# Attention with pooled keys, then an MLP: the first batch loaded and turned one head pair at a time

## The chip, the cores and the metric

The kernel runs on one core of a Trainium2 chip. The metric is device microseconds of one execution, taken as the median of several. Before the change it is 308.15 us (4 runs, 307.08 to 308.27). The engines are TensorE (PE; PEld is its weight load), VectorE (DVE), ScalarE (ACT), GpSimd (POOL) and SyncE (SP), which only issues DMAs here. Each engine runs its own instructions in order, and waits on semaphores for the others. ACT and POOL issue DMAs too, each on a queue of its own; all queues are served by the same 16 DMA engines. A load that POOL issues may convert float32 to bfloat16 on the way.

## The reference

Eight batches of 8 heads, 576 positions, head dimension 64. Keys and values are averaged over groups of 8 positions, so that each head has 72 of them; softmax attention follows, and its output (4608 tokens of 512 features) goes through an MLP with hidden size 2048 and the activation h - tanh(h).

```python
k_p = k.reshape(B, H, Sp, pool, D).mean(axis=3)      # 576 -> 72 rows
v_p = v.reshape(B, H, Sp, pool, D).mean(axis=3)
scores = scale * np.matmul(q, k_p.transpose(0, 1, 3, 2))
attn = softmax(scores)
x = np.matmul(attn, v_p)                             # then heads side by side
h = x @ w_in                                         # (4608, 512) @ (512, 2048)
out = (h - np.tanh(h)) @ w_out                       # (4608, 2048) @ (2048, 512)
```

## The kernel before

**Layout of k and v.** Two heads make a pair; a pair has 2 x 72 = 144 pooled rows (`PR`). The pair t, of four (`NM`), puts its first 128 rows in `k_raw[:, t, :]`, one row per partition, eight positions of 64 numbers each. The 16 rows left over (`LO`) of all four pairs share a fifth slice, `k_raw[:, NM, :]`: pair t has partitions 32t to 32t+15, the others hold zero. `v_raw` has the same layout. `load_main` (L101) loads the main rows, `load_left` (L105) the leftover rows, with one DMA per pair.

**Pooling.** `pool_k` (L186 to L194) adds the eight positions in three steps and writes the sum twice, side by side, into `kd`. TensorE turns `kd` by a matmul with the identity (`turn_tile`, L243), and `kb_main` and `kb_left` copy the result out of PSUM into `KB` so that two heads share a 128-column block with zeros where they must not meet. `VB` is built from pooled v: each pair's rows are written twice, multiplied by a mask that keeps the one or the other head (`v_spread`, L216 and L224); its last column holds the pool size, so that the attention matmul gives the softmax denominator too.

**Attention of a batch.** `score_mms` (L282) multiplies a block of `KB` with the turned q of that pair; the leftover rows of all pairs make a fifth tile, each pair in its 32 partitions. The exponential goes into `E` (L312). `av_half` (L330) gives 128 tokens of four heads: two matmuls for the two pairs, a third for their leftover rows. A reciprocal and a product on VectorE make `x_sb` (L343, L344). `x_pe_transpose` (L374) turns it into `xT` (copy on ScalarE, L381), the MLP's input.

**The MLP.** Tokens go in 9 groups of 512. `mlp_h_mms` (L412) accumulates one of 16 hidden blocks over four feature blocks, so heads 0-3 give the first two of them and heads 4-7 the last two; `mlp_h_act` takes tanh on ScalarE (L423) and the difference on VectorE (L425). `mlp_o` (L440) is the second layer. While TensorE works on group g, GpSimd pools k and v of a later batch and casts q.

**What sets the order.** The order of each engine's instructions is that of the program text, written out by hand (`manual_schedule`). Waits are placed by the framework, from the tiles that an instruction reads and writes. Two more kinds of waits matter here. DMAs take their completion semaphores in turn from a small set of lanes (eight for SP and ACT together, eight for POOL), so a DMA waits for the one that used its lane before. And `after` adds waits by hand: batch 1's k loads wait for the second of four chunks of `w1`.

**The start.** Batch 0 has nothing to hide behind. SP loads k pairs 0 and 1, the four leftover pieces, then pairs 2 and 3; ACT loads q in two halves; POOL loads v as bfloat16 straight into `v_bf` (a view of `v_raw[0]`), then `w1` in four chunks and the first of `w2`. VectorE pools k, TensorE turns k and q, pools v by eight matmuls with the identity as weights (L596), and multiplies zeros in between (`warm_pe`, L511), results of which nobody reads. The MLP's first matmuls on batch 0 are those of the first two feature blocks of hidden blocks 0 to 4. Then come group 0's remaining hidden blocks; group 0's second layer (16 steps u) is interleaved with the attention of batch 1: its k is turned after u=0 (`k_transpose`), its q from u=3, and `av` starts at u=9.

Of the kernel before, what the change touches and what calls it, by code (L numbers as in the profile page):

```python
# [8 lines left out]
FP32 = mybir.dt.float32  # L9
BF16 = mybir.dt.bfloat16  # L10
# [27 lines left out]
def kernel(  # L38
# [34 lines left out]
    xT = const.tile([128, NFB, T], BF16, name="xT")  # L73
    ident = const.tile([128, 128], BF16, name="ident")
    mask = const.tile([128, 3 * NM, 1], FP32, name="mask")
    k_raw = [const.tile([128, NT, POOL * D], FP32, name=f"k_raw{i}") for i in range(2)]
# [26 lines left out]
    def load_left(src, dst, b):  # L103
# [3 lines left out]
        ]  # L107

    def load_k(b):
        return [load_main(k_pairs, k_raw[b % 2], b, 0, NM)] + load_left(  # L110
            k_pairs, k_raw[b % 2], b
        )

# [88 lines left out]
    def pool_v(b, eng):  # L202
        r = v_raw[b % 2].rearrange("p t (j d) -> p t j d", d=D)
        eng.tensor_tensor(  # L204
            out=r[:, :, 0:4, :], in0=r[:, :, 0:4, :], in1=r[:, :, 4:8, :], op=ALU.add
        )
        eng.tensor_tensor(  # L207
            out=r[:, :, 0:2, :], in0=r[:, :, 0:2, :], in1=r[:, :, 2:4, :], op=ALU.add
        )
        eng.tensor_tensor(  # L210
            out=r[:, :, 0, :], in0=r[:, :, 0, :], in1=r[:, :, 1, :], op=ALU.add
        )
        v_spread(VB[b % 2], r[:, :, 0:1, :], eng)

    def v_spread(vb, vs, eng):
        eng.tensor_tensor(  # L216
            out=vb[:, 0 : 2 * NM, 0:D].rearrange("p (t s) d -> p t s d", s=2),
            in0=vs[:, 0:NM, :, :].to_broadcast([128, NM, 2, D]),
            in1=mask[:, 0 : 2 * NM, :]
            .rearrange("p (t s) o -> p t s o", s=2)  # L220
            .to_broadcast([128, NM, 2, D]),
            op=ALU.mult,
        )
        eng.tensor_tensor(  # L224
            out=vb[:, 2 * NM :, 0:D],
            in0=vs[:, NM, :, :].to_broadcast([128, NM, D]),
            in1=mask[:, 2 * NM :, :].to_broadcast([128, NM, D]),
            op=ALU.mult,
        )
# [6 lines left out]
    def kb_left(kb, ps, eng):  # L236
        eng(
            out=kb[D:128, :].rearrange("p (t x) -> p t x", x=KP)[:, :, 128 : 128 + LO],
            in_=ps[D:128, :].rearrange("p (t x) -> p t x", x=32)[:, :, 0:LO],
        )  # L240
# [35 lines left out]

    def score_mms(b, t, dst, c0, c1):
        for m in range(NM) if t == NM else (t,):
            o = m * KP + (128 if t == NM else 0)
# [25 lines left out]
    def scores_wide(b, ts):  # L305
# [3 lines left out]
        for t in ts:  # L309
            ps = ps_any([128, QA], FP32, "s_ps")  # L310
            score_mms(b, t, ps[:, :], 0, QA)
            nc.scalar.activation(out=E[:, t, 0:QA], in_=ps[:, :], func=ACT.Exp, scale=SCALE)  # L312

    def scores_tail(b):
        ps = ps_any([128, NT, QT], FP32, "s_ps")
        for t in range(NT):
            score_mms(b, t, ps[:, t, :], QA, S)
        nc.scalar.activation(
            out=E_tiles[b][:, :, QA:S], in_=ps[:, :, :], func=ACT.Exp, scale=SCALE
        )  # L320

    def av_half(b, blk, half, x_sb, alloc):
        E = E_tiles[b]
# [3 lines left out]
        for n in range(3):  # L327
            t = 2 * half + n if n < 2 else NM
            s0 = 2 * t if n < 2 else 2 * NM + 2 * half
            nc.tensor.matmul(  # L330
                ps[:, 2 * n : 2 * n + 2, :].rearrange("p h d -> p (h d)")
                if n < 2
                else ps.rearrange("p (a s) d -> p a s d", s=2)[:, :, 1, :],
                lhsT=E[:, t, c0 : c0 + 128],
                rhs=vb[:, s0 : s0 + 2, :].rearrange("p h d -> p (h d)")
                if n < 2
                else vb[:, s0 : s0 + 2, :],
                start=(n == 0),
# [185 lines left out]
    nc.vector.memset(k_raw[0][:, NM, :], 0.0)  # L524
    load_main(k_pairs, k_raw[0], 0, 0, 2)
    load_q0(0, 4)
    load_left(k_pairs, k_raw[0], 0)
    load_main(k_pairs, k_raw[0], 0, 2, 4)
    load_q0(4, 8)
    nc.scalar.dma_start(out=t0[:QT, :, R, :], in_=q[0, :, QA:S, :].rearrange("h p d -> p h d"))  # L530

    warm_pe(13)
    nc.vector.memset(warm[:, :], 0.0)
# [3 lines left out]
    make_identity(nc, ident)  # L537
    nc.gpsimd.memset(v_bf[:, NM, :], 0.0)
    nc.gpsimd.memset(q_bf[64:128, R, :, :], 0.0)
# [18 lines left out]
    nc.gpsimd.dma_start(out=v_bf[:, 0:NM, :], in_=v_pairs[0, 0:128, :, :])  # L558
    for t in range(NM):
        nc.gpsimd.dma_start(  # L560
            out=v_bf[32 * t : 32 * t + LO, NM, :], in_=v_pairs[0, 128:PR, t, :]
        )
    for c in range(4):
        load_w1(c)
    load_w2(0)
    nc.gpsimd.memset(k_raw[1][:, NM, :], 0.0)
    nc.gpsimd.memset(v_raw[1][:, NM, :], 0.0)
    nc.gpsimd.memset(v_raw[0][:, NM, :], 0.0)
# [16 lines left out]

    pool_k(0, nc.vector, 0, 2)
    def q_turn(eng, h0, h1):
# [5 lines left out]
    def v_pe_pool():  # L593
        ps = ps_any([128, NT, 1, D], FP32, "v_ps")
        for j in range(POOL):
            nc.tensor.matmul(  # L596
                ps[:, :, 0, :],
                lhsT=ident[:, :],
                rhs=v_bf[:, :, j * D : (j + 1) * D],
                start=(j == 0),  # L600
                stop=(j == POOL - 1),
            )
        v_spread(VB[0], ps, nc.vector)

# [3 lines left out]
    ps_all = ps_any  # L608
    q_turn(nc.vector.tensor_copy, 0, 4)
    k_turn(0, 2)  # L610
    warm_pe(1)
    q_pe_transpose(0, (0, 1), "act")
    pool_k(0, nc.vector, 4, 5)
    pool_k(0, nc.vector, 2, 4)
    warm_pe(3)
    scores_wide(0, (0, 1))
    q_turn(nc.scalar.copy, 4, 8)
    warm_pe(5)
    k_turn_left()
    k_turn(2, 4)  # L620
    q_pe_transpose(0, (2, 3), "act")
    v_pe_pool()
    scores_wide(0, (2, 3, 4))
    xs = [new_x() for _ in range(4)]
    gts = []
    warm_pe(2)
    av_half(0, 0, 0, xs[0], ps_all)
    av_half(0, 1, 0, xs[1], ps_all)
    warm_pe(1)
    x_pe_transpose(0, 0, xs[0], (0, 2))  # L630
    av_half(0, 2, 0, xs[2], ps_all)
    warm_pe(1)
    x_pe_transpose(0, 1, xs[1], (0, 2))
    av_half(0, 3, 0, xs[3], ps_all)
    warm_pe(1)
    x_pe_transpose(0, 2, xs[2], (0, 2))
    ps_any = ps_b1
    av_half(0, 0, 1, xs[0], ps_any)
    warm_pe(1)
    x_pe_transpose(0, 3, xs[3], (0, 2))  # L640
    av_half(0, 1, 1, xs[1], ps_any)
    av_half(0, 2, 1, xs[2], lambda sh, dt, name: ps_h.tile(sh, dt, name=name, tag="hT_ps"))
    mlp_h_mms(0, 0, 0, 2)
    x_pe_transpose(0, 0, xs[0], (2, 4))
    av_half(0, 3, 1, xs[3], ps_any)
    mlp_h_mms(0, 1, 0, 2)
    x_pe_transpose(0, 1, xs[1], (2, 4))
    mlp_h_mms(0, 2, 0, 2, (ps_o, "o_ps"))
    x_pe_transpose(0, 2, xs[2], (2, 4))
    mlp_h_mms(0, 3, 0, 2, (ps_o, "o_ps"))  # L650
    mlp_h_mms(0, 4, 0, 2)
    x_pe_transpose(0, 3, xs[3], (2, 4))
# [115 lines left out]
```

The softmax here doesn't subtract the row's maximum and nothing guards it: scores larger than these inputs give would overflow.

## Time and profile before

| | |
|---|---|
| median of 4 runs | 308.15 us |
| profiled execution | 308.21 us |
| its span, first to last instruction | 306.3 us |
| PE busy | 290.6 us, 95% |
| DVE, ACT, POOL busy | 51%, 47%, 41% |
| mean granted TensorE clock | 0.986 |
| DMA | 49.73 MB, mean 162 GB/s |
| first matmul of the MLP (L412) | 25.46 us |
| first matmul of its second layer (L440) | 42.57 us |

The profile comes from one execution. Its page cuts the span into 40 equal slices and gives the busy share of each engine in tenths, the TensorE clock that the throttle granted, and what the DMA engines moved. The chain of waits follows back from the last instruction, step by step, to what released it. Groups of instructions and waits are named by line of the kernel and by tile. An instruction's line can be that of a helper. A load's time to landing runs from its issue to its completion semaphore.

In the first 50 us the DMA engines move 12.33 MB, counted as written (a converting load reads twice that). The median times from issue to landing there: first half of k 4.4 us, second half 8.5, the two halves of q 6.4, v's main rows 8.4, v's leftover pieces 7.3, `w1` chunks 11.9, the leftover pieces of k 6.8.

### The profile page before, as it was taken

What the parts mean: (1) busy time and instruction counts of PE and PEld (TensorE: products, weight loads), DVE (VectorE), ACT (ScalarE), POOL (GpSimd) and SP (SyncE); (2) the same over time, 40 slices, a digit from 0 to 9 for tenths busy, and PEclk for the clock granted to TensorE, in tenths of its full rate; (3) what the DMA queues carried; (4) which work ended last, traced back from release to release, by engine and by line L of the source; (5) the groups of instructions that cost most, each with busy time, mean ns of one, the idle gap of its engine ahead of it and who ended that gap; (6) DMA issues with size and microseconds to landing.
All of it is one profiled execution on the core that took longest, in us unless ns stands there. A gap on an engine that the chain in (4) does not pass through costs nothing.

```text
span 306.3 us, 4667 instructions
## 1 busy us (share of the span) xinstructions
PE 290.6 (95%) x1631; PEld 142.8 (47%) x1662; DVE 155.0 (51%) x333; ACT 145.1 (47%) x276; POOL 127.0 (41%) x120
## 2 busy tenths in 40 slices
PE   6379999999999999999999999999999999999995
PEld 2145445644454445444544454445444544444443
DVE  4245861767175716571658165816572557207700
ACT  1436745366515651566157615661566146226511
POOL 8610995981089302980794049703980000000000
PEclk9969999999999999999999999999999999999998
DMA  7999999556955599559855985699641640111032
GB/s 230 232 207 297 256 210 291 177 156 173 323 126 107 130 298 252 115 169 324 161 109 125 327 220 118 161 300 210 112 83 34 71 112 0 36 68 34 1 69 70
DMA packets 66583, 49.73 MB, mean 162 GB/s; under 512 B 40320, under 2 KB 53440, under 8 KB 66560
## 3 DMA queue, kind: packets, MB, share of 16 engines
q1 hardware_dynamic: 59936, 43.34, 56.1%
q0 software_dynamic: 4880, 4.78, 9.6%
q10 hardware_dynamic: 1744, 1.31, 1.5%
q8 instruction: 13, 0.21, 0.3%
q14 instruction: 10, 0.08, 0.1%
HBM read 36.70 MB, written 9.44 MB: 151 GB/s over the span
## 4 chain that ended last, share of the span: by engine, by line
PE 89%; DMA 5%; DVE 2%; issue 1%; ACT 1%; SPq 0%
PE o_ps L440 39%; PE hT_ps L412 39%; PE x_ps L330 4%; PE s_ps L282 4%; DMA k_raw<-in_k_dram 3%; DMA q_raw<-in_q_dram 2%; DVE gT L425 1%; PE xT_ps L374 1%; DMA out_dram<-o_sb 1%; PE v_ps L596 1%; PE qT_ps L159 1%; DVE x_sb L344 0%; ACT t_sb L423 0%; PE warm_ps L511 0%; ACT xT L381 0%
## 5 line engine op out<-in xcount | busy, mean ns | idle before, releaser
L440 PE MATMUL o_ps<-w2b,gT 128*128 128x512 bf16 x542 | 132.0, 379 | 1.2 <-issue 0.3
L412 PE MATMUL hT_ps<-xT,w1b 128*128 128x512 bf16 x564 | 126.4, 379 | 1.6 <-ACT xT L381 0.5
L425 DVE TENSOR_TENSOR gT<-hT_ps,t_sb 128x512 bf16<-128x512 f32 x144 | 98.9, 690 | 56.8 <-ACT t_sb L423 56.7
L423 ACT ACTIVATE t_sb<-hT_ps 128x512 f32<-128x512 f32 x144 | 85.6, 597 | 38.6 <-PE hT_ps L412 38.2
L412 PEld LDWEIGHTS <-w1b 128*128 128x128 bf16 x576 | 55.8, 98 | 67.2 <-issue 1.8
L440 PEld LDWEIGHTS <-gT 128*128 128x128 bf16 x560 | 52.5, 98 | 52.0 <-issue 1.4
L449 ACT COPY o_sb<-o_ps 128x512 f32<-128x512 f32 x33 | 19.3, 585 | 75.2 <-PE o_ps L440 72.3
L343 DVE RECIPROCAL rden<-x_ps 128x4 f32<-128x4 f32 x80 | 14.1, 176 | 55.1 <-PE x_ps L330 54.7
L137 POOL CAST q_bf<-q_raw 128x2048 bf16<-128x2048 f32 x7 | 13.2, 1890 | 60.7 <-issue 35.5
L344 DVE TENSOR_TENSOR x_sb<-x_ps,rden 128x256 bf16<-128x256 f32 x80 | 33.9, 424 | 5.9 <-DMA xT<-x_sb 2.8
L301 ACT ACTIVATE E<-s_ps 128x288 bf16<-128x288 f32 x60 | 21.4, 410 | 13.2 <-PE s_ps L282 13.0
L186 POOL TENSOR_TENSOR k_raw<-k_raw 128x1280 f32<-128x1280 f32 x7 | 20.2, 2884 | 17.7 <-DMA k_raw<-in_k_dram 17.7
L330 PE MATMUL x_ps<-VB,E 128*128 128x130 bf16 x240 | 21.0, 220 | 0.0
L330 PEld LDWEIGHTS <-E 128*128 128x128 bf16 x240 | 16.9, 98 | 8.3 <-ACT E L312 0.2
L204 POOL TENSOR_TENSOR v_raw<-v_raw 128x1280 f32<-128x1280 f32 x7 | 20.3, 2900 | 0.0
L282 PE MATMUL s_ps<-qT,KB 128*128 128x288 bf16 (+5 forms) x128 | 17.4, 300 | 0.1
L282 PEld LDWEIGHTS <-KB 128*128 128x128 bf16 (+1 forms) x128 | 7.2, 97 | 10.8 <-issue 4.2
L207 POOL TENSOR_TENSOR v_raw<-v_raw 128x640 f32<-128x640 f32 x7 | 10.8, 1543 | 0.6
L189 POOL TENSOR_TENSOR k_raw<-k_raw 128x640 f32<-128x640 f32 x7 | 10.8, 1539 | 0.5
L194 POOL TENSOR_TENSOR kd<-k_raw 128x640 bf16<-128x640 f32 x7 | 10.8, 1540 | 0.5
L511 PE MATMUL warm_ps<-xT 128*128 128x512 bf16 x27 | 8.8, 444 | 1.5 <-DVE xT L523 1.3
L381 ACT CAST xT<-xT_ps 128x256 bf16<-128x256 f32 (+1 forms) x14 | 6.1, 434 | 7.7 <-PE xT_ps L374 7.5
(66 smaller groups left out, 98.6 us busy)
## 6 DMA issues: line engine op xcount, KB each, us to landing
k_raw<-in_k_dram SPq DMA_DIRECT2D x7, 1024.0 KB, 6.5
q_raw<-in_q_dram SPq DMA_DIRECT2D x7, 1024.0 KB, 7.2
v_raw<-in_v_dram SPq DMA_DIRECT2D x7, 1024.0 KB, 8.5
out_dram<-o_sb SPq DMA_DIRECT2D x38, 128.0 KB, 2.4
out_dram<-o_sb SPq DMA_DIRECT2D x16, 256.0 KB, 2.6
w1b<-in_moe_w_in_dram POOLq DMA_DIRECT2D x4, 512.0 KB, 11.9
w2b<-in_moe_w_out_dram POOLq DMA_DIRECT2D x4, 512.0 KB, 5.9
k_raw<-in_k_dram SPq DMA_DIRECT2D x2, 512.0 KB, 6.5
```

The source lines that it names most:

```text
L186: first = eng.tensor_tensor(out=r[:, :, 0:4, :], in0=r[:, :, 0:4, :], in1=r[:, :, 4:8, :], op=ALU.add)
L204: eng.tensor_tensor(out=r[:, :, 0:4, :], in0=r[:, :, 0:4, :], in1=r[:, :, 4:8, :], op=ALU.add)
L282: nc.tensor.matmul(dst[p : p + w], lhsT=KB[b % 2][:, o : o + w], rhs=qTs[b][:, m, c0:c1], start=True, stop=True,)
L301: nc.scalar.activation(out=E[:, t, half * hs : (half + 1) * hs], in_=ps[:, :], func=ACT.Exp, scale=SCALE)
L330: nc.tensor.matmul(ps[:, 2 * n : 2 * n + 2, :].rearrange("p h d -> p (h d)") if n < 2 else ps.rearrange("p (a s) d -> p a s d", s=2)[:, :, ...
L343: nc.vector.reciprocal(out=rden[:, :, :], in_=ps[:, :, D:D1])
L344: nc.vector.tensor_tensor(out=x_sb[:, half, :, :], in0=ps[:, :, 0:D], in1=rden[:, :, :].to_broadcast([128, 4, D]), op=ALU.mult,)
L412: nc.tensor.matmul(h_tiles[i][:, :], lhsT=w1b[:, fb, i * 128 : (i + 1) * 128], rhs=xT[:, fb, tok0 : tok0 + TG], start=(fb == 0), stop=(fb ...
L423: nc.scalar.activation(out=t_sb[:, :], in_=h_ps[:, :], func=ACT.Tanh)
L425: nc.vector.tensor_sub(out=gT[:, :], in0=h_ps[:, :], in1=t_sb[:, :])
L440: nc.tensor.matmul(o_ps[:, :], lhsT=gts[i][:, tb * 128 : (tb + 1) * 128], rhs=w2b[:, i, :], start=(i == 0), stop=(i == NHID - 1),)
L449: (nc.vector.tensor_copy if g == 0 and tb % 2 else nc.scalar.copy)(out=o_sb[:, :], in_=o_ps[:, :])
```

## The change

It touches batch 0's start, and the leftover rows of k in every batch.

- The leftover rows of k come in one DMA (`load_dense`) into partitions 0 to 63, 16 per pair without a space between them; `kb_left` reads them at that distance. This holds for every batch. Leftover rows of v keep their four DMAs from batch 1 on.
- For batch 0, the leftover rows of v come in one DMA from SP too, as float32 into `v_raw[1]`; GpSimd copies them to `v_bf`. A new constant `spread`, the identity with its columns set 32 apart, is the weight of eight more matmuls that pool these rows and put them at 32t. Main rows are pooled by eight matmuls with `ident`, as before. `v_spread` becomes `v_main` and `v_left`; batch 0 writes heads 0-3, then the leftover rows, then heads 4-7.
- Loads of k and q for pairs 0 and 1 come one pair each, and are pooled, cast and turned one by one; ACT casts three of q's four pieces and VectorE the last. k's pairs 2 and 3 follow the dense load on SP.
- The first chunk of `w1` waits for k's last load (`after`); the copy of v's leftover rows stands on GpSimd between it and the other chunks.
- Scores of the leftover rows are taken in two halves (`scores_left`): heads 0-3 before k's pairs 2 and 3 are turned, heads 4-7 with them. `av_half` then takes, for batch 0, the 64 partitions of its own half alone. Some PSUM tiles come from other pools.
- The filler matmuls are 24 instead of 27 and stand in other places.

```diff
--- before.py
+++ after.py
...
     ident = const.tile([128, 128], BF16, name="ident")
+    spread = const.tile([128, 128], BF16, name="spread")
     mask = const.tile([128, 3 * NM, 1], FP32, name="mask")
...
+    def load_dense(src, dst, b):
+        return nc.sync.dma_start(
+            out=dst[0 : NM * LO, NM, :], in_=src[b, 128:PR, :, :].rearrange("p t n -> t p n")
+        )
+
     def load_k(b):
-        return [load_main(k_pairs, k_raw[b % 2], b, 0, NM)] + load_left(
-            k_pairs, k_raw[b % 2], b
-        )
+        return [
+            load_main(k_pairs, k_raw[b % 2], b, 0, NM),
+            load_dense(k_pairs, k_raw[b % 2], b),
+        ]
...
         )
-        v_spread(VB[b % 2], r[:, :, 0:1, :], eng)
-
-    def v_spread(vb, vs, eng):
+        v_main(VB[b % 2], r[:, :, 0:1, :], eng, 0, NM)
+        v_left(VB[b % 2], r[:, :, 0:1, :], eng)
+
+    def v_main(vb, vs, eng, t0, t1):
+        n = t1 - t0
         eng.tensor_tensor(
-            out=vb[:, 0 : 2 * NM, 0:D].rearrange("p (t s) d -> p t s d", s=2),
-            in0=vs[:, 0:NM, :, :].to_broadcast([128, NM, 2, D]),
-            in1=mask[:, 0 : 2 * NM, :]
+            out=vb[:, 2 * t0 : 2 * t1, 0:D].rearrange("p (t s) d -> p t s d", s=2),
+            in0=vs[:, t0:t1, :, :].to_broadcast([128, n, 2, D]),
+            in1=mask[:, 2 * t0 : 2 * t1, :]
             .rearrange("p (t s) o -> p t s o", s=2)
-            .to_broadcast([128, NM, 2, D]),
+            .to_broadcast([128, n, 2, D]),
             op=ALU.mult,
         )
+
+    def v_left(vb, vs, eng):
         eng.tensor_tensor(
...
             out=kb[D:128, :].rearrange("p (t x) -> p t x", x=KP)[:, :, 128 : 128 + LO],
-            in_=ps[D:128, :].rearrange("p (t x) -> p t x", x=32)[:, :, 0:LO],
+            in_=ps[D:128, 0 : NM * LO].rearrange("p (t x) -> p t x", x=LO),
         )
...
-    def score_mms(b, t, dst, c0, c1):
-        for m in range(NM) if t == NM else (t,):
+    def score_mms(b, t, dst, c0, c1, pairs=range(NM)):
+        for m in pairs if t == NM else (t,):
             o = m * KP + (128 if t == NM else 0)
...
+    def scores_left(b, half):
+        ps = ps_any([128, QA], FP32, "s_ps")
+        score_mms(b, NM, ps, 0, QA, (2 * half, 2 * half + 1))
+        r = slice(64 * half, 64 * half + 64)
+        nc.scalar.activation(out=E_tiles[b][r, NM, 0:QA], in_=ps[r, :], func=ACT.Exp, scale=SCALE)
+
     def scores_tail(b):
...
-    def av_half(b, blk, half, x_sb, alloc):
+    def av_half(b, blk, half, x_sb, alloc, own=False):
         E = E_tiles[b]
...
             s0 = 2 * t if n < 2 else 2 * NM + 2 * half
+            r = slice(64 * half, 64 * half + 64) if own and n == 2 else slice(0, 128)
             nc.tensor.matmul(
...
                 else ps.rearrange("p (a s) d -> p a s d", s=2)[:, :, 1, :],
-                lhsT=E[:, t, c0 : c0 + 128],
+                lhsT=E[r, t, c0 : c0 + 128],
                 rhs=vb[:, s0 : s0 + 2, :].rearrange("p h d -> p (h d)")
                 if n < 2
-                else vb[:, s0 : s0 + 2, :],
+                else vb[r, s0 : s0 + 2, :],
                 start=(n == 0),
...
     nc.vector.memset(k_raw[0][:, NM, :], 0.0)
-    load_main(k_pairs, k_raw[0], 0, 0, 2)
-    load_q0(0, 4)
-    load_left(k_pairs, k_raw[0], 0)
-    load_main(k_pairs, k_raw[0], 0, 2, 4)
+    nc.vector.memset(v_raw[1][:, NM, :], 0.0)
+    load_main(k_pairs, k_raw[0], 0, 0, 1)
+    load_q0(0, 2)
+    load_main(k_pairs, k_raw[0], 0, 1, 2)
+    load_q0(2, 4)
+    load_dense(k_pairs, k_raw[0], 0)
     load_q0(4, 8)
+    k_last = load_main(k_pairs, k_raw[0], 0, 2, 4)
+    load_dense(v_pairs, v_raw[1], 0)
     nc.scalar.dma_start(out=t0[:QT, :, R, :], in_=q[0, :, QA:S, :].rearrange("h p d -> p h d"))
-    warm_pe(13)
+    warm_pe(9)
     nc.vector.memset(warm[:, :], 0.0)
...
     make_identity(nc, ident)
-    nc.gpsimd.memset(v_bf[:, NM, :], 0.0)
     nc.gpsimd.memset(q_bf[64:128, R, :, :], 0.0)
...
     nc.gpsimd.dma_start(out=v_bf[:, 0:NM, :], in_=v_pairs[0, 0:128, :, :])
-    for t in range(NM):
-        nc.gpsimd.dma_start(
-            out=v_bf[32 * t : 32 * t + LO, NM, :], in_=v_pairs[0, 128:PR, t, :]
-        )
-    for c in range(4):
-        load_w1(c)
+    nc.gpsimd.memset(spread[:, :], 0.0)
+    nc.gpsimd.tensor_copy(
+        out=spread.rearrange("p (t x) -> p t x", x=32)[:, :, 0:LO],
+        in_=ident[:, 0 : NM * LO].rearrange("p (t x) -> p t x", x=LO),
+    )
+    load_w1(0)
+    after(w1_dmas, k_last)
+    nc.gpsimd.tensor_copy(out=v_bf[:, NM, :], in_=v_raw[1][:, NM, :])
+    load_w1(1)
+    load_w1(2)
+    load_w1(3)
     load_w2(0)
     nc.gpsimd.memset(k_raw[1][:, NM, :], 0.0)
-    nc.gpsimd.memset(v_raw[1][:, NM, :], 0.0)
     nc.gpsimd.memset(v_raw[0][:, NM, :], 0.0)
...
-    pool_k(0, nc.vector, 0, 2)
+    pool_k(0, nc.vector, 0, 1)
+    pool_k(0, nc.vector, 1, 2)
     def q_turn(eng, h0, h1):
...
         ps = ps_any([128, NT, 1, D], FP32, "v_ps")
-        for j in range(POOL):
-            nc.tensor.matmul(
-                ps[:, :, 0, :],
-                lhsT=ident[:, :],
-                rhs=v_bf[:, :, j * D : (j + 1) * D],
-                start=(j == 0),
-                stop=(j == POOL - 1),
-            )
-        v_spread(VB[0], ps, nc.vector)
+        for t0, t1, turn in ((0, NM, ident), (NM, NT, spread)):
+            for j in range(POOL):
+                nc.tensor.matmul(
+                    ps[:, t0:t1, 0, :],
+                    lhsT=turn[:, :],
+                    rhs=v_bf[:, t0:t1, j * D : (j + 1) * D],
+                    start=(j == 0 and t0 == 0),
+                    stop=(j == POOL - 1),
+                    skip_group_check=True,
+                )
+        v_main(VB[0], ps, nc.vector, 0, 2)
+        v_left(VB[0], ps, nc.vector)
+        v_main(VB[0], ps, nc.vector, 2, 4)
...
     ps_all = ps_any
-    q_turn(nc.vector.tensor_copy, 0, 4)
-    k_turn(0, 2)
+    q_turn(nc.scalar.copy, 0, 2)
+    q_turn(nc.scalar.copy, 2, 4)
+    k_turn(0, 1)
+    q_pe_transpose(0, (0,), "act")
     warm_pe(1)
-    q_pe_transpose(0, (0, 1), "act")
-    pool_k(0, nc.vector, 4, 5)
+    k_turn(1, 2)
+    q_pe_transpose(0, (1,), "act")
+    warm_pe(2)
+    scores_wide(0, (0, 1))
+    q_turn(nc.scalar.copy, 4, 6)
+    warm_pe(2)
+    pool_k(0, nc.vector, NM, NT)
+    k_turn_left()
     pool_k(0, nc.vector, 2, 4)
+    q_turn(nc.vector.tensor_copy, 6, 8)
+    warm_pe(1)
+    scores_left(0, 0)
     warm_pe(3)
-    scores_wide(0, (0, 1))
-    q_turn(nc.scalar.copy, 4, 8)
-    warm_pe(5)
-    k_turn_left()
     k_turn(2, 4)
...
     v_pe_pool()
-    scores_wide(0, (2, 3, 4))
+    warm_pe(1)
+    scores_wide(0, (2, 3))
+    scores_left(0, 1)
     xs = [new_x() for _ in range(4)]
     gts = []
+    ps_o2 = lambda sh, dt, name: ps_o.tile(sh, dt, name=name, tag="o_ps")
+    ps_h2 = lambda sh, dt, name: ps_h.tile(sh, dt, name=name, tag="hT_ps")
     warm_pe(2)
-    av_half(0, 0, 0, xs[0], ps_all)
-    av_half(0, 1, 0, xs[1], ps_all)
-    warm_pe(1)
+    av_half(0, 0, 0, xs[0], ps_all, True)
+    av_half(0, 1, 0, xs[1], ps_all, True)
+    av_half(0, 2, 0, xs[2], ps_all, True)
     x_pe_transpose(0, 0, xs[0], (0, 2))
-    av_half(0, 2, 0, xs[2], ps_all)
+    av_half(0, 3, 0, xs[3], ps_all, True)
     warm_pe(1)
     x_pe_transpose(0, 1, xs[1], (0, 2))
-    av_half(0, 3, 0, xs[3], ps_all)
+    ps_any = ps_b1
+    av_half(0, 0, 1, xs[0], ps_h2, True)
     warm_pe(1)
     x_pe_transpose(0, 2, xs[2], (0, 2))
-    ps_any = ps_b1
-    av_half(0, 0, 1, xs[0], ps_any)
+    av_half(0, 1, 1, xs[1], ps_b1, True)
     warm_pe(1)
     x_pe_transpose(0, 3, xs[3], (0, 2))
-    av_half(0, 1, 1, xs[1], ps_any)
-    av_half(0, 2, 1, xs[2], lambda sh, dt, name: ps_h.tile(sh, dt, name=name, tag="hT_ps"))
+    av_half(0, 2, 1, xs[2], ps_o2, True)
     mlp_h_mms(0, 0, 0, 2)
     x_pe_transpose(0, 0, xs[0], (2, 4))
-    av_half(0, 3, 1, xs[3], ps_any)
+    av_half(0, 3, 1, xs[3], ps_b1, True)
     mlp_h_mms(0, 1, 0, 2)
     x_pe_transpose(0, 1, xs[1], (2, 4))
-    mlp_h_mms(0, 2, 0, 2, (ps_o, "o_ps"))
+    mlp_h_mms(0, 2, 0, 2)
+    mlp_h_mms(0, 3, 0, 2, (ps_o, "o_ps"))
     x_pe_transpose(0, 2, xs[2], (2, 4))
-    mlp_h_mms(0, 3, 0, 2, (ps_o, "o_ps"))
-    mlp_h_mms(0, 4, 0, 2)
+    mlp_h_mms(0, 4, 0, 2, (ps_o, "o_ps"))
     x_pe_transpose(0, 3, xs[3], (2, 4))
...
     for i in range(5):
```

## The prediction

> **What bounds the kernel now.** I read the page first: the row of busy shares by slice, with the granted clock under it.
>
> ```profile
> PE   6379999999999999999999999999999999999995
> ...
> PEclk9969999999999999999999999999999999999998
> ```
>
> TensorE is 90% busy or more in every slice but the first three (some 7.7 us each) and the last, where the output drains. So only the first 23 us hold time that a rearranged start can give back. Next, the chain of waits from 0 to 60 us:
>
> ```profile
> 0.81 5.50 DMA q_raw<-in_q_dram
> 6.31 0.02 issue
> 6.33 8.49 DMA k_raw<-in_k_dram
> ...
> 14.85 0.70 DVE k_raw L186
> ...
> 16.52 0.40 PE kT_ps L243 x2
> 16.91 0.85 PE qT_ps L159 x8
> 17.76 2.13 PE v_ps L596 x8
> 19.90 1.40 PE s_ps L282 x6
> ...
> 25.46 0.59 PE hT_ps L412 x2
> ```
>
> The set-off is a load, not arithmetic: head pairs 2 and 3 of k are issued only at 6.33, when a q load has landed, and land at 14.82. All TensorE work behind them is serial. The waits of SP's queue name the cause:
>
> ```profile
> SPq L101 <- DMA w1b<-in_moe_w_in_dram: 12.5, 1, 12.5
> ...
> SPq L101 <- DMA q_raw<-in_q_dram: 2.3, 1, 2.3
> ```
>
> The 2.3 us wait is a semaphore lane: that k load reuses the lane of the first q load. The 12.5 us wait is by design: batch 1's k waits for the second w1 chunk, which landed at 19.3. Third, the stage table, in stretches in which the clock is constant:
>
> ```profile
> 7.70:11.10 3.40, 2.78 (x18) 1.17 (x16) 1.16 (x4) 3.09 (x5) 2.17 (x3) 1.00 1.24 215
> 11.10:14.50 3.40, 0.23 (x1) 0.10 (x1) 0.12 (x1) 0.00 (x0) 1.64 (x3) 1.00 1.18 257
> 14.50:17.90 3.40, 1.39 (x12) 1.27 (x13) 2.35 (x6) 0.53 (x2) 1.87 (x4) 0.50 1.24 206
> 17.90:21.30 3.40, 3.40 (x14) 1.32 (x14) 1.02 (x2) 1.49 (x4) 0.00 (x0) 0.50 1.24 206
> ```
>
> (After the length: busy PE, PEld, DVE, ACT, POOL; clock; DMA share; GB/s.) TensorE is idle for nearly all of 11.1 to 14.5, and the next two stretches run at clock 0.50. The wait is thus paid twice. Last, what stands behind an earlier start: GpSimd's preparation of batch 1, and the TensorE work that takes it.
>
> ```profile
> 30.54 2.90 POOL L186 TENSOR_TENSOR k_raw<-k_raw 128x1280 f32<-128x1280 f32 x1 [14.17 <-DMA k_raw<-in_k_dram]
> ...
> 35.81 1.55 POOL L194 TENSOR_TENSOR kd<-k_raw 128x640 bf16<-128x640 f32 x1
> ...
> 39.92 0.61 POOL L140 CAST q_bf<-q_raw 64x512 bf16<-64x512 f32 x1
> ```
>
> ```profile
> 43.44 0.44 PE L243 MATMUL kT_ps<-ident,kd 128*128 128x128 bf16 x5
> ...
> 46.30 0.61 PE L159 MATMUL qT_ps<-ident,q_bf 128*128 128x128 bf16 x8
> ```
>
> kd is done at 37.36 and used at 43.44 (6.1 us spare); q is cast at 40.53 and used at 46.30 (5.8). VB of batch 1 ends at 48.4, its first use is at 54.3 (5.9). So batch 1 has 5.8 us of slack in all three: a start earlier by more than that runs into GpSimd.
>
> **The change part by part.**
>
> *k's second half (the gain).* In the built order this load carries no lane wait any more: SP issues two 256 KB loads, the dense rest (it waits for the memset of k_raw, done at 1.74) and then this load. With 0.39 to 0.46 us per issue that is about 2.2 instead of 6.33. Landing after issue: 4.4 us for the first k load, which had little beside it; 6.4 the median of the two q loads; 8.5 for this very load, beside GpSimd's v load; 12.0 the longest load of its line. I take 8.5, the load nearest in size and company: 10.7, against 14.82. Ends: 8.6 and 14.2. Gain 4.1 us (6.2 to 0.6).
>
> *Clock.* TensorE would wait from about 10.9 (early scores, three fillers) to 12.3 (10.7 plus 1.6 for the three DVE adds): 1.4 us, not 5.0. The stretch 4.3 to 7.7 was busy 2.07 of 3.40 and no drop followed; 0.23 of 3.40 was followed by one. I therefore take clock 1.00 for kT, qT, v_ps and s_ps: 0.40+0.85+2.13+1.40 = 4.78 becomes 2.4. Gain 2.4; at the other end 0.
>
> *Order on TensorE.* The scores of the rest rows of heads 0-3 move ahead of the second half, so the first attention matmul no longer waits for the exponentials: 21.99 less the end of its fillers, some 0.3. v is pooled in 16 matmuls instead of 8 with the same columns, +0.1. Fillers: 24 instead of 27, but one more stands behind v (+0.2, 0.22 being a 512-column matmul in the steady rows). DVE writes VB in three pieces, the first two (2 x 0.42) before attention instead of 0.69+0.42: 0.2 earlier. Together -0.2, from -0.5 to +0.3. The pooling of the rest and q's casts (ACT 0.5 each, DVE 0.4) lie before 10.7 or beside the q transposes; if k came at 8.6 the rest's 1.0 us of DVE would be uncovered.
>
> *Rest rows of v (a new wait).* SP issues them when the first q load lands (about 5.3); queued behind it there is only batch 1, which waits until 19 anyway. They go in the ring behind k's second half, landing from 11.5 to 15; then a GpSimd copy (0.55, as the memset of the same tile) and the spread matmuls. TensorE reaches these at about 14.0, so the delay is 0 to 1.5 us; I take 0.5. Removed from GpSimd: four issues (2.43 us) and a 0.52 memset; added: spread's memset and copy, some 0.4.
>
> *w1 (late on purpose).* The first chunk is issued at 10.7 instead of 7.57. A weight chunk issued into an empty queue lands in 5.8 (the w2 chunk at 35.0): 16.5, against a first use near 19.7. The copy of v's rest, and a wait for its DMA, now stands before the other four weight issues on GpSimd's queue. The second chunk is then issued by 11.5 to 15.5, landing between 19.1 (one 2.6 us transfer after the first) and 21.3, against 19.3 before. Its use in front of hidden unit 4 is near 22. So TensorE is covered, but batch 1's k, which waits for that chunk on SP, moves by -0.2 to +2.0; I take +0.7. One rest DMA instead of four (1.84 us of issue at 19.8) gives SP's queue back about 1.4, which q and v of batch 1 use; none of it is on the path.
>
> *Later batches.* Three issues fewer per k load on SP, off the path: nothing, as TensorE has no gap there. If the cover failed, I bound it at half a microsecond either way.
>
> **Sum.** Front: 4.1 + 2.4 + 0.2 - 0.5 = 6.2 us. Batch 1 lets through 5.8 - 0.7 = 5.1. The smaller holds: 5.1 us. The profiled execution took 308.21 (span 306.3 and 1.9 around it), 0.06 above the median of 308.15. 308.2 - 5.1 = 303.1.
>
> [...] The trace shows the rest's old form (16 rows a DMA) landing 5.6 to 9.8 us after issue, and nothing of a 64-row one. [...]
>
> **The rivals.**
> - *The load stays late* (bandwidth, not the lane, sets k's second half). For: the DMA share is above 1 from 5 us on. Against: the wait is 2.3 us and q alone filled the queues before it. At 13.0 instead of 10.7 the front gives 3.9: 304.3; at 14.2 with the slow clock 0.6 less the v wait: 308.
> - *Batch 1 late*: the second w1 chunk at 21.3 or later, so k of batch 1 at 33 instead of 30.5. 5.8 - 2.5 = 3.3: 304.9, TensorE waiting in kT_ps near 39.
> - *Slower than before*: the same wait, longer. GpSimd stands at v's rest copy, w1's chunks 1 to 3 queue behind it, and batch 1 behind chunk 1. It decides where chunk 1 lands later than 19.3 + 5.8 = 25.1, that is v's rest at about 18.7. At 21 it costs 2.3: 310.5. Against: 128 KB queued from 5.3 on, where the slowest landing row is 13.2 (18.5).
> - *More*: k at 8.6 and batch 1 no later or earlier by a microsecond, since its rest is one DMA: 6.2 to 6.8, 301.4 to 302.
>
> **How the numbers follow.** Forecast (302.3 to 304.1) 0.50; load late 0.15; batch 1 late 0.13; more 0.10; slower 0.08; no change 0.04. Leaving out slower, no change and the last part of more: 301.6 to 306.2. 0.3% is 0.9 us, about what a measurement of this kernel tells from no change. Faster: 0.50+0.15+0.13+0.10, less a little for a late load that falls near 308, 0.87; same 0.04; slower 0.09.
>
> **What the profile after would show.** Right: k's second half issued near 2.2 and landing near 10.7; no slice at clock 0.50 after the first; first hT_ps near 19.7; kT_ps of batch 1 waiting a little for kd near 38. Wrong: a wait of v_ps for spread past 15.5, or of POOL's copy; w1b waited for by hT_ps; kT_ps waiting beyond 39; a clock of 0.50 in the second or third slice.

## The result, and the profile after

The changed kernel takes 309.27 us (median of 33 runs, 306.93 to 311.22), the kernel before 307.85 (52 runs, 306.52 to 308.56): a ratio of 1.0046, 95% interval 1.0034 to 1.0058. It is slower by half a per cent; 303.1 was predicted, and the range ended at 306.2. The profiled execution took 310.49 us, with a span of 308.8 (before: 308.21 and 306.3). It ran 1.2 us above its median, so the two profiles differ by 2.5 us where the medians differ by 1.4.

The page of the kernel after: busy tenths of TensorE by slice, and the clock granted.

```profile
span 308.8 us, 4654 instructions
...
PE   8599999999897999999999999999999999999995
...
PEclk9669999999999999999999999999999999999999
```

The first three slices are busier than before (8, 5, 9, where they were 6, 3, 7), but two of them run at a lowered clock instead of one, and matmuls take longer there (the four score matmuls of 512 columns at 19.22 take 1.60 us; in e7, where the clock is at 1.00, 0.92). New are the 8 and 7 in slices eleven and thirteen, about 77 to 100 us, where before TensorE was at 9 throughout. The chain of waits has another load at its head:

```profile
3.68 12.98 DMA v_raw<-in_v_dram
16.66 0.04 issue
16.70 2.29 PE v_ps L623 x16
19.00 0.22 issue
19.22 1.60 PE s_ps L293 x4
...
25.24 0.59 PE hT_ps L430 x2
```

The main rows of v, issued at 3.68, land 12.98 us later, at 16.66; before they took 8.4 us. The first MLP matmul starts at 25.24; before it was 25.46. So of the 6.2 us that the front (the time up to this matmul) was to give, 0.2 came. The timeline of VectorE shows k landing (time, duration, line, in brackets the wait ahead and for whom):

```profile
10.65 0.42 DVE L193 TENSOR_TENSOR k_raw<-k_raw 128x256 f32<-128x256 f32 x1 [3.61 <-DMA k_raw<-in_k_dram]
...
13.36 0.69 DVE L193 TENSOR_TENSOR k_raw<-k_raw 128x512 f32<-128x512 f32 x1 [1.02 <-DMA k_raw<-in_k_dram]
```

The first line is k's dense rest, issued at 1.77; the second is pairs 2 and 3, issued at 2.54. The lane wait is gone, as predicted: this load has semaphore 108, which no load before it used, where in the kernel before it had 100, that of the first q load, which landed at 6.31. But from the issue of this load to its pooling it is 10.8 us, where 8.5 to landing was predicted. The stage table, in the stretches shown of before:

```profile
7.70:11.10 3.40, 0.88 (x4) 0.19 (x2) 0.42 (x1) 1.10 (x3) 0.00 (x0) 0.92 1.20 218
11.10:14.50 3.40, 2.65 (x7) 0.51 (x7) 1.92 (x5) 1.21 (x2) 0.75 (x1) 0.50 0.55 115
14.50:17.90 3.40, 2.44 (x16) 1.93 (x17) 1.35 (x5) 1.07 (x2) 1.45 (x3) 0.50 0.97 139
17.90:21.30 3.40, 3.18 (x20) 1.43 (x18) 1.09 (x3) 1.39 (x3) 3.40 (x6) 0.58 1.01 156
```

The clock falls to 0.50 about 4 us earlier than before (at 10.55 instead of 14.52) and comes back at about the same time (20.79 and 21.35). And in 11.1 to 14.5, while three loads are waited for, the DMA engines work at less than half of what they did in that stretch before: share 0.55 and 115 GB/s, against 1.18 and 257. The loads are late although the DMA engines, taken together, have room. Last, GpSimd's timeline:

```profile
13.63 0.75 POOL L505 DMA_DIRECT2D w1b<-in_moe_w_in_dram  x1 [8.46 <-DMA k_raw<-in_k_dram]
16.45 0.61 POOL L587 CAST v_raw<-v_raw 128x512 bf16<-128x512 f32 x1 [2.08 <-DMA v_raw<-in_v_dram]
17.01 2.23 POOL L505 DMA_DIRECT2D w1b<-in_moe_w_in_dram  x3
...
35.63 2.90 POOL L193 TENSOR_TENSOR k_raw<-k_raw 128x1280 f32<-128x1280 f32 x1 [14.09 <-DMA k_raw<-in_k_dram]
...
59.16 2.90 POOL L193 TENSOR_TENSOR k_raw<-k_raw 128x1280 f32<-128x1280 f32 x1 [5.70 <-DMA k_raw<-in_k_dram]
```

In the kernel before, the pooling of batch 2's k stood here:

```profile
51.90 2.89 POOL L186 TENSOR_TENSOR k_raw<-k_raw 128x1280 f32<-128x1280 f32 x1 [3.51 <-DMA k_raw<-in_k_dram]
```

SP issues batch 1's k, which waits for the second `w1` chunk, at 22.38 instead of 19.32. Batch 1's k is pooled 5.1 us later (35.63 against 30.54), and batch 2's 7.3 later (59.16 against 51.90). TensorE's timeline shows where that comes out:

```profile
78.30 0.42 PE L293 MATMUL s_ps<-qT,KB 128*128 128x288 bf16 x2 [0.79 <-POOL KB L245]
...
95.50 1.67 PE L430 MATMUL hT_ps<-xT,w1b 128*128 128x512 bf16 x6 [1.76 <-DMA xT<-x_sb]
```

These are two waits of together 2.6 us, both on the way of batch 2's attention; before, TensorE had neither of them. From the first MLP matmul to the end of the span it is 308.8 - 25.24 = 283.6 us, before 306.3 - 25.46 = 280.8. In these two executions the change is thus a front that gained 0.2 us and a later part that lost 2.7.

### The profile page after: what moved, and what is told of

The parts are those of the page before. It is cut to its first block, busy times and chain, and to the rows that moved or that the text cites. A ratio compares the mean times of both kernels' runs of the same rounds, so it can differ in the third digit from the quotient of the medians.

```text
span 308.8 us, 4654 instructions
## 1 busy us (share of the span) xinstructions
PE 293.9 (95%) x1635; PEld 144.0 (47%) x1666; DVE 155.9 (51%) x340; ACT 146.6 (47%) x279; POOL 124.6 (40%) x117
## 4 chain that ended last, share of the span: by engine, by line
PE 86%; DMA 6%; POOL 3%; issue 2%; DVE 1%; SPq 1%; ACT 1%; POOLq 0%
PE o_ps L458 38%; PE hT_ps L430 37%; PE x_ps L348 5%; DMA v_raw<-in_v_dram 4%; PE s_ps L293 4%; POOL v_raw L211 1%; DMA xT<-x_sb 1%; DMA out_dram<-o_sb 1%; PE xT_ps L392 1%; PE v_ps L623 1%; POOL v_raw L214 1%; SPq L379 0%; PE warm_ps L529 0%; POOL VB L225 0%; PE qT_ps L166 0%
## 5 line engine op out<-in xcount | busy, mean ns | idle before, releaser
L348 PE MATMUL x_ps<-VB,E 128*128 128x130 bf16 (+1 forms) x240 | 21.8, 221 | 0.0
L348 PEld LDWEIGHTS <-E 128*128 128x128 bf16 (+1 forms) x240 | 17.2, 98 | 9.1
L293 PEld LDWEIGHTS <-KB 128*32 128x32 bf16 (+1 forms) x128 | 7.2, 97 | 12.4 <-issue 4.3
L529 PE MATMUL warm_ps<-xT 128*128 128x512 bf16 x23 | 9.8, 539 | 1.3 <-DVE xT L541 1.3
L214 POOL TENSOR_TENSOR v_raw<-v_raw 128x640 f32<-128x640 f32 x7 | 10.8, 1544 | 0.5
L201 POOL TENSOR_TENSOR kd<-k_raw 128x640 bf16<-128x640 f32 x7 | 10.8, 1545 | 0.5
L196 POOL TENSOR_TENSOR k_raw<-k_raw 128x640 f32<-128x640 f32 x7 | 10.8, 1538 | 0.5
## 6 DMA issues: line engine op xcount, KB each, us to landing
v_raw<-in_v_dram SPq DMA_DIRECT2D x7, 1024.0 KB, 10.2
```

What stands on the lines that cost most here:

```text
L293: nc.tensor.matmul(dst[p : p + w], lhsT=KB[b % 2][:, o : o + w], rhs=qTs[b][:, m, c0:c1], start=True, stop=True,)
L348: nc.tensor.matmul(ps[:, 2 * n : 2 * n + 2, :].rearrange("p h d -> p (h d)") if n < 2 else ps.rearrange("p (a s) d -> p a s d", s=2)[:, :, ...
```

## The experiments

Two measures are given of each kernel: the ratio to the kernel before on the same chip, and from its one profile the start of the first MLP matmul ("front") and the time from there to the end of the span ("rest"). Single executions scatter by up to 2.3 us about their median, so the ratio decides on size and the profile on place. Kernels with the same front differ in it by about 1 us from profile to profile (25.24, 24.73 and 24.16 in the changed kernel, e4 and e6).

| kernel | ratio, 95% interval | median us | front | rest |
|---|---|---|---|---|
| before | 1 | 307.85 | 25.46 | 280.8 |
| after | 1.0046 (1.0034 to 1.0058) | 309.27 | 25.24 | 283.6 |
| e1: 16 rows outermost | 0.9919 (0.9886 to 0.9952) | 305.23 | 21.31 | 280.7 |
| e2: before, k's rest dense, pairs outermost | 0.9985 (0.9963 to 1.0008) | 307.34 | 23.02 | 283.2 |
| e3: before, k's rest dense, rows outermost | 0.9859 (0.9824 to 0.9895) | 303.52 | 21.73 | 280.8 |
| e4: copy of v's rest later | 1.0045 (1.0018 to 1.0072) | 309.06 | 24.73 | 283.1 |
| e5: rows outermost in batch 0 only | 0.9983 (0.9969 to 0.9997) | 306.97 | 21.86 | 283.4 |
| e6: rows outermost from batch 1 on | 0.9972 (0.9957 to 0.9987) | 306.53 | 24.16 | 280.6 |
| e7: e1 with 8 more fillers | 0.9875 (0.9858 to 0.9893) | 303.79 | 20.23 | 282.3 |
| e8: e3 with 7 more fillers | 0.9849 (0.983 to 0.9867) | 302.83 | 20.32 | 280.8 |
| e9: e7, `w1` not held back | 0.9837 (0.9809 to 0.9864) | 302.61 | 20.67 | 280.7 |
| e10: before, k ahead of its rest | 0.9938 (0.992 to 0.9956) | 305.81 | 22.85 | 280.9 |

**e1: the order inside the dense loads.** A dense load names its 64 rows of 2 KB with the four pairs outermost. The theory, a supposition of the author's when it was put down, is that such a load runs on four DMA engines; what the traces show of it stands below. The edit is in `load_dense`, so it holds for both dense loads of batch 0 (k's and v's rest) and for that of k in each later batch. It names the same 64 rows with the 16 rows outermost; they land in another order, which the reader of the PSUM tile and `spread` follow.

```diff
-            out=dst[0 : NM * LO, NM, :], in_=src[b, 128:PR, :, :].rearrange("p t n -> t p n")
+            out=dst[0 : NM * LO, NM, :], in_=src[b, 128:PR, :, :]
...
-            in_=ps[D:128, 0 : NM * LO].rearrange("p (t x) -> p t x", x=LO),
+            in_=ps[D:128, 0 : NM * LO].rearrange("p (x t) -> p t x", t=NM),
```

> The changed kernel with one thing undone: the two dense loads put the 16 rows outermost instead of the four pairs (partition 4p+t instead of 16t+p; the copy into KB and the spread matrix follow). Same bytes, same number of DMAs, same places in the queues. Theory F (the dense loads ran on four of the 16 DMA engines, and everything queued on those four came late): k's rest, which landed at 10.6, lands by 8.5; k's second half, 13.4, by 11; v's main rows, 16.7, by 13; first hT_ps from 25.2 to 19.5 to 22; no clock of 0.50 beyond 15; total 302.5 to 305.5. Rival B (bandwidth: 3.5 MB must come before the MLP whatever their order): the same landings within a microsecond, k's second half at 12.5 or later, total 308.5 to 310.

VectorE's timeline of e1:

```profile
7.67 0.43 DVE L193 TENSOR_TENSOR k_raw<-k_raw 128x256 f32<-128x256 f32 x1 [0.67 <-DMA k_raw<-in_k_dram]
...
10.22 0.69 DVE L193 TENSOR_TENSOR k_raw<-k_raw 128x512 f32<-128x512 f32 x1 [0.92 <-DMA k_raw<-in_k_dram]
```

The DMA view of e1, of what was issued in the first 6 us (KB of each, median us from issue to landing):

```profile
k_raw<-in_k_dram SPq DMA_DIRECT2D x1, 512.0 KB, 7.7
v_raw<-in_v_dram POOLq DMA_DIRECT2D x1, 512.0 KB, 9.5
k_raw<-in_k_dram SPq DMA_DIRECT2D x1, 128.0 KB, 5.9
...
v_raw<-in_v_dram SPq DMA_DIRECT2D x1, 128.0 KB, 6.7
```

The rest is pooled 3.0 us earlier than in the changed kernel, k's second half 3.1, and the main rows of v, loaded in another queue, land after 9.5 us instead of 13.0. Both waits of batch 2 are gone. The order inside the dense loads turns a loss of 0.5% into a gain of 0.8%. The landings, the front and the total came as theory F had them (v's main rows at 13.15 for 13), but not the clock: it is at 0.50 from 12.7 to 16.1, where none was expected beyond 15. The profile of e1 is of its fastest run (303.68 us, median 305.23), so its front may flatter it.

The two orders differ in the trace too. It records each update that a DMA makes on its completion semaphore, of which the views use only the last. In the seven traces of before, after, e1, e2, e3, e5 and e6, every load of k, q, v and `w1` issued in the first 56 us makes 16 updates, except the dense loads with pairs outermost. Each of those makes five: one about 1 us after the issue, and four at the end.

| updates of the semaphore, us | changed kernel | e1 |
|---|---|---|
| k's rest, issued at 1.77 | 2.89; 9.46, 9.77, 9.89, 10.62 | 16, from 6.25 to 7.65 |
| k's second half, issued at 2.54 (e1 2.49) | 12 up to 11.02; 12.27, 12.50, 12.55, 13.34 | 16, from 9.63 to 10.20 |
| main rows of v, issued at 3.68 (e1 3.69) | 12 up to 14.30; 15.34, 15.54, 15.91, 16.66 | 16, from 12.46 to 13.15 |

So in the changed kernel the last four of the 16 updates of the other two loads are what comes late. The DMA view of the changed kernel from 14 to 15 us agrees (packets, MB, share of 16 engines):

```profile
q0 software_dynamic: 24, 0.02, 13.9%
q1 hardware_dynamic: 20, 0.04, 11.5%
q10 hardware_dynamic: 12, 0.00, 1.4%
```

Together these are 26.8% of 16 engines, or 4.3 engines; in e1 the queue of GpSimd alone shows 125.5% in that microsecond. The trace does not name the engines: that four of them carried the dense loads fits these numbers, but was not shown.

**e2 and e3: k's dense load alone.** The kernel before, with nothing but `load_dense` for k, in every batch (and the reader of the PSUM tile to match), in the change's order (e2) and in e1's (e3).

```diff
     load_q0(0, 4)
-    load_left(k_pairs, k_raw[0], 0)
+    load_dense(k_pairs, k_raw[0], 0)
     load_main(k_pairs, k_raw[0], 0, 2, 4)
```

> The kernel before with one part of the change alone: the rest rows of k in one DMA, pairs outermost (16 columns per pair in kb_left), in every batch. It takes three DMAs out of the lanes, so k's second half no longer waits for q's load. Theory F: the rest lands at 9.5 to 11.5 and drags k's second half, issued near 2.3, to 11.5 to 13.5 instead of 14.8; w1 is not held back, so batches 1 and 2 come as before; total 305.5 to 307.5. Rival S (dense loads in the later batches are what delays batch 2): stalls of TensorE near 78 and 95 like those after the change, total 308.5 to 310.

> The same as the run before it, but with the 16 rows outermost. Theory F: the rest lands by 8.5, k's second half near 9.5 to 11, first hT_ps near 21 to 22.5, total 303.5 to 306, some 1 to 3 us below the run with pairs outermost. Rival B: equal to that run within 0.5 us.

e3 is at least as fast as the whole of e1, with a small part of its edit. Between e2 and e3 there is only the order of k's dense load, and it is worth 1.3% here as well. In e2 the front gains 2.4 us, k's second half being pooled at 12.81 (e3: 10.68), and the rest of the program loses as much: 283.2, with a wait of 1.9 us for `xT` again. So the later loss comes with the pairs-outermost load alone, without any part of the new order of batch 0. The total of e2 lies in the range of its theory F, but its words that batches 1 and 2 come as before were wrong.

**e4: is it GpSimd standing at the copy?** This is the prediction's "slower" rival. The copy of v's rest goes behind the `w1` chunks.

```diff
     after(w1_dmas, k_last)
-    nc.gpsimd.tensor_copy(out=v_bf[:, NM, :], in_=v_raw[1][:, NM, :])
     load_w1(1)
     load_w1(2)
     load_w1(3)
+    nc.gpsimd.tensor_copy(out=v_bf[:, NM, :], in_=v_raw[1][:, NM, :])
```

> The changed kernel with GpSimd's copy of v's rest moved behind the issue of w1's chunks 1 to 3 (all still behind k's second half). Theory C (the added 2.5 us is the wait of that copy in front of the weight chunks, passed on by batch 1's k to batch 2's preparation, and met by TensorE near 78 and 95): the second w1 chunk lands at 19.5 to 20.5 instead of 22.4, batch 1's pooling starts at 32 to 34 instead of 35.6, TensorE's waits for POOL's KB copy (0.8) and for xT's DMA (1.8) shrink below 1 in sum, the front stays as it was (first hT_ps 25 to 26), total 306.5 to 308. Rival S (the stalls near 78 and 95 come from the new form of the later batches' loads): the two waits stay above 2 in sum, total 308.8 to 309.8.

Batch 1's k is pooled 1.5 us earlier (34.18), batch 2's 1.9 (57.29), but the two late waits stay (1.6 and 0.4 us), and the time is the same as the changed kernel's. So the copy's place delays weights, but it does not set the end.

**e5 and e6: which loads cost what.** The rows-outermost order in batch 0 alone (e5), or in all batches but that (e6).

```diff
-            out=dst[0 : NM * LO, NM, :], in_=src[b, 128:PR, :, :].rearrange("p t n -> t p n")
+            out=dst[0 : NM * LO, NM, :],
+            in_=src[b, 128:PR, :, :] if b == 0 else src[b, 128:PR, :, :].rearrange("p t n -> t p n"),
```

(e6 has `b > 0`; in both, the readers of the rows follow.)

> The changed kernel with the 16 rows outermost in batch 0's two dense loads only; later batches keep the four pairs outermost. Theory S (the new load form slows batches 1 and 2 by itself): first hT_ps near 21.3 as in the run with 16 everywhere, but batch 1's pooling starts at 33 or later and TensorE waits 1 to 3 us near 75 and 92; total 306 to 307.5. Theory C (batches 1 and 2 are late only because the start was late): no such waits, total 304 to 305.5.

> The counterpart: pairs outermost in batch 0, the 16 rows outermost from batch 1 on. Theory S: front as after the change (first hT_ps near 25), batch 1's pooling at 33.5 to 34.5 instead of 35.6, the waits near 78 and 95 gone or under 1 us in sum, total 306.8 to 307.8. Theory C: waits of 2 us and more stay, total 308.7 to 309.7.

TensorE's waits in e5, after 40 us:

```profile
PE hT_ps L431 <- DMA xT<-x_sb: 1.5, 1, 1.5
...
PE s_ps L294 <- POOL KB L246: 0.3, 1, 0.3
PE kT_ps L255 <- POOL kd L202: 0.3, 1, 0.3
```

In e6 none of these three is left. The order in batch 0 sets the front (21.9 against 24.2), that in the later batches the rest (283.4 against 280.6). By the ratios the first is worth 0.6%, the second 0.7%, and both together 1.3%. In e5 the front is e1's within 0.6 us, and still batch 1's k is pooled at 33.18 instead of 31.35, batch 2's at 55.48 instead of 53.16. So about half of the loss is no echo of the late front; the later loads make it themselves. Batch 1's dense load shows how: it is issued at 20.63 in e5 and 20.12 in e1, makes its last update at 33.01 and 31.18, and the pooling starts 0.17 us after that. And e6 shows the converse: its front is late, and its rest loses nothing (its total, 306.53, came 0.3 us below the range of theory S).

**e10: the lane wait by itself.** In the kernel before, two lines change places, so that k's second half takes a free lane and the last rest piece the busy one.

```diff
     load_q0(0, 4)
-    load_left(k_pairs, k_raw[0], 0)
     load_main(k_pairs, k_raw[0], 0, 2, 4)
+    load_left(k_pairs, k_raw[0], 0)
     load_q0(4, 8)
```

> The kernel before with two lines exchanged: k's second half is issued in front of the four pieces of its rest, nothing else. Theory (the semaphore lane, not bandwidth, held k's second half): it is issued near 1.3 and its DMA lands at 8 to 10 instead of 14.8; the last piece of the rest takes over the wait for q's load, and the VectorE pools the rest first, so that the second half is pooled at 12 to 13.5; total 305.3 to 307. Rival B (bandwidth sets it): pooled at 14 or later, total 307.3 to 308.5.

The DMA issues of SP in e10, from its timeline:

```profile
0.81 0.97 SPq L101 DMA_DIRECT2D k_raw<-in_k_dram  x2
1.82 4.67 SPq L105 DMA_DIRECT2D k_raw<-in_k_dram  x4
```

The last piece of the rest now waits instead: the four take 4.67 us to issue, where it was 2.21 before. The rest is pooled at 11.91 and k's second half right behind it at 12.90, where it was at 14.85 before. The front is 2.6 us earlier, the time 0.6% less. The prediction's reading of the lane was right.

**e7 and e8: the clock.** In e1 TensorE still waits 1.73 us for k's second half, and the clock falls. e7 puts fillers in that wait, e8 does the same to e3.

```diff
     scores_left(0, 0)
-    warm_pe(3)
+    warm_pe(11)
     k_turn(2, 4)
```

```diff
     k_turn_left()
+    warm_pe(7)
     k_turn(2, 4)
```

> The run with the 16 rows outermost everywhere, with 11 filler matmuls instead of 3 between the early scores of the rest rows and the turn of k's second half. Theory: there TensorE was idle for 1.7 us and more and the clock fell to 0.50 from 12.7 to 16.1, which doubled q's and v's matmuls; with the fillers the clock stays at 1.00 and first hT_ps comes at 19.3 to 20.3 instead of 21.3; total 302.5 to 304.5 if batch 1 follows. Rival (GpSimd's preparation of batches 1 and 2 holds what the front gains): first hT_ps earlier all the same, waits in kT_ps or s_ps instead, total 304.5 to 305.5.

> The kernel before with k's rest in one DMA, 16 rows outermost, and seven more filler matmuls behind the turn of the rest rows. Theory: no clock of 0.50 from 13.2 to 16.6, first hT_ps at 19.5 to 20.8 instead of 21.7, total 301.8 to 303. Rival: v's main rows (0.8 us waited for) and GpSimd take it back, total 303 to 304.

The stage table of e1, in stretches that follow its clock:

```profile
5.90:9.30 3.40, 2.73 (x14) 0.93 (x13) 2.27 (x9) 2.79 (x6) 0.00 (x0) 1.00 1.10 308
9.30:12.70 3.40, 1.61 (x11) 0.64 (x11) 2.41 (x5) 1.08 (x2) 2.16 (x4) 1.00 1.15 202
12.70:16.10 3.40, 3.27 (x23) 2.35 (x23) 1.06 (x5) 1.17 (x2) 3.40 (x6) 0.50 1.06 162
```

and of e7:

```profile
9.30:12.70 3.40, 3.10 (x15) 1.10 (x14) 2.16 (x5) 0.59 (x1) 1.73 (x3) 1.00 1.19 197
12.70:16.10 3.40, 3.22 (x32) 2.08 (x34) 2.24 (x6) 1.91 (x4) 3.40 (x6) 1.00 1.06 161
```

Busy 3.10 instead of 1.61 of 3.40, and the next stretch keeps clock 1.00. v's main matmuls take 1.04 us instead of 1.92. The front is 1.1 us earlier in e7 and 1.4 in e8; the medians fall by 1.4 and 0.7 us, but with intervals that overlap those of e1 and e3, so the profile shows the effect on the front, and the times only agree with it. In e7 a part is lost again: TensorE waits 1.4 us for a chunk of `w2`.

**e9: is `w1` better held back?** e7 without the added wait of `w1`'s first chunk on k's last load.

```diff
     load_w1(0)
-    after(w1_dmas, k_last)
```

> The run with 16 rows outermost and 11 fillers, without the wait of w1's first chunk for k's second half. Theory (the hold keeps the queues free for k and v): the chunk is issued near 5.2 and shares the DMA engines with k's second half, which lands at 11.3 to 12.5 instead of 10.7; v's main rows are waited for; first hT_ps at 20.7 to 22 instead of 20.2; total 303.8 to 305. Rival (the hold only makes weights late; TensorE waited 1.4 us for a w2 chunk with it): k's second half within half a microsecond, batch 1's pooling a microsecond earlier, no wait for w2b, total 302.2 to 303.3.

The first chunk is issued at 5.13; k's second half is pooled at 11.17, half a microsecond later than in e7 (10.70), and batch 1's k at 30.18 instead of 30.97. The wait for `w2` is gone and the rest is 280.7 again. So the theory failed and its rival held. The median is 1.2 us lower, and the intervals overlap. e9 and e8 are the best, 302.61 and 302.83, and not told apart. e8 is the kernel before with k's dense load, rows outermost, and seven fillers; it comes out level with the whole change in that order, with more fillers and without the hold on `w1`.

## Why the prediction was wrong

Two of its steps failed. The later batches were put at nothing and lost 2.7 us. The front was to give 6.2 us and gave 0.2, as the loads behind and beside the dense loads came late and the clock stayed low. Most of both comes from the order inside the dense loads: with rows outermost (e1) the front gives 4.2 us by its one profile and the later part loses nothing. Term by term:

- *k's second half, the issue.* This was right: it is issued at 2.54, predicted was 2.2, and e10 shows that moving the lane wait alone is worth 0.6%.
- *Its landing.* This was mis-sized. The prediction took 8.5 us from the row of before; measured were 10.8, and the pooling starts at 13.36 instead of 14.85 before, so 1.5 of the 4.1 us came. e1, with 7.7 us and pooling at 10.22, shows that the row was a fair choice but for the rest load ahead, in the order that it had: between e1 and the changed kernel that order is 3.1 us, for which the sum has no term.
- *Main rows of v.* This step is missing. The prediction put TensorE at v's rest rows near 14.0 and gave no wait for the main rows, which had taken 8.4 us before. They took 13.0, and became the head of the chain.
- *Clock.* "I therefore take clock 1.00" failed. TensorE waited 3.20 us for the rest's `kd`, and then 0.60 for k's second half, and the clock was 0.50 from 11.1 to 17.9. By the rows of TensorE's timeline, kT, qT, v and scores took 0.40+1.06+2.49+1.60 = 5.55 us, and before 0.40+1.06+2.34+1.61 = 5.41, so none of the 2.4 us came. (The prediction's 4.78 counts the same work before without the overlaps.) Even the forecast wait of 1.4 us was not surely safe: after e1's 1.73 us the clock fell.
- *Rest rows of v.* The spread matmuls stand behind v's main ones without a wait of their own, so the 0.5 us was not paid there; the copy's wait of 2.08 us held up `w1`.
- *w1.* The second chunk was to come 0.7 us later (at most 2.0); it came 3.06 later. Batch 1's k then takes 13.25 us from issue to pooling instead of 11.22 (in e1 11.70). Together these are the 5.1 us.
- *Batch 1's slack of 5.8 us.* This was right: q's cast ends at 45.61, the first q matmul stands at 45.85, and TensorE waits for nothing there.
- *"Later batches: nothing, as TensorE has no gap there."* This failed. The rest loses 2.7 us, and 2.6 in e5, where "half a microsecond either way" was the bound; it is what makes the kernel slower rather than equal. The step counted the issues that SP is spared, not how long the new load takes to land: batch 1's is issued at 22.85 and makes its last update at 35.47, 12.6 us later, where the four pieces took 9.2 to 9.8 before.
- *The rivals.* "Slower" named a chain that is there (copy, `w1`, batch 1), but chunk 1 came at 22.38, before its bound of 25.1, and e4 shows that the copy is not the price. "The load stays late" gave the front's size best: landing near 13 with the slow clock. None put a late front and late batches on the same cause, and so the range ended at 306.2. The prediction noted that the trace showed nothing of a 64-row load, and gave such a load no term in the sum; by e1, e2 and e3 the order inside it decided the case.

Two things stay open: how the delay of the later batches' loads reaches the two waits of batch 2, which was not followed step by step, and whether e8 or e9 is faster.

## What to carry to other kernels

When several DMAs are merged into one, look at the outermost dimension, of the source too: the destination had 64 partitions in both orders here, and still the same 64 rows of 2 KB cost 1.3% of this kernel with 4 outermost and 16 inside, against 16 outermost. Price such a load wherever it recurs, and on all that is in flight beside it, other queues too (3.5 us on v's load in GpSimd's queue here), not only on its own reader. And where TensorE still waits a microsecond or two at the start, try fillers in that wait: in e7 and e8 they kept the clock at 1.00 and brought the front 1.1 and 1.4 us.

## What the runs showed of the hardware

Not expected: two loads of 128 KB held up loads of 512 KB, one in SP's queue by 3.1 us (10.8 to landing instead of 7.7) and one in GpSimd's by 3.5 (13.0 instead of 9.5; the changed kernel against e1), while the share of the DMA engines fell to 0.55 (the changed kernel, 11.10 to 14.50). With k's load alone (e2 against e3) it was 2.1 us, and 1.3 in the other queue (10.2 us to landing instead of 8.9). The held-up loads had 12 of their 16 semaphore updates early and four late (k's second half 12 up to 11.02 and four from 12.27 to 13.34, v's main rows 12 up to 14.30 and four from 15.34 to 16.66).

TensorE's clock fell to 0.50 after a stretch of 3.4 us with 1.61 us busy (e1, 9.30 to 12.70) and one with 1.48 (the changed kernel, 7.10 to 10.50), not only after a nearly idle one (0.23 busy in the kernel before, 11.10 to 14.50). A fall came after a wait of 1.73 us in e1, and within one of 3.20 us in the changed kernel (8.58 to 11.78, the fall at 10.55). None came after the wait of 1.22 us in the kernel before, at 6.93, nor in e8, whose longest wait in that part is 0.82 us.
